# Direct head transposes, mask columns on VectorE and a reordered hand-over between two batches in a fused attention and snake-MLP kernel

## The chip, the cores and the metric

The kernel runs on one core of a Trainium2 chip. A core has a matrix engine (TensorE, PE in the profile, with its weight loads shown as PEld), VectorE (DVE), ScalarE (ACT), GpSimd (POOL) and SyncE (SP), each with an instruction queue of its own, and 16 DMA engines for transfers. The metric is the device time of one execution in microseconds. Before the change its median is 237.07 us over 8 runs (236.63 to 237.79).

## The reference

Four batches, 8 heads, 768 positions, head size 64. Each position attends to 8 memory keys of its batch and head and to a window around its own chunk of 32 positions; the result of all heads goes through a two-layer MLP with a snake activation.

```python
for c in range(nc):                       # chunks of 32
    l_start = max(0, c_start - 16); r_end = min(S, c_end + 8)
    k_full = np.concatenate([mem_k, k[:, :, l_start:r_end]], axis=2)
    v_full = np.concatenate([mem_v, v[:, :, l_start:r_end]], axis=2)
    scores = scale * np.matmul(q_c, k_full.transpose(0, 1, 3, 2))
    a = softmax(scores)
    out[:, :, c_start:c_end] = np.matmul(a, v_full)
x = out.transpose(0, 2, 1, 3).reshape(B * S, H * D)
h = x @ w_in                              # 512 -> 2048
s = np.sin(alpha * h)
g = h + s * s / (alpha + 1e-09)
return (g @ w_out).astype(np.float32)     # 2048 -> 512
```

## The kernel before

The work goes batch by batch, and the order of every engine's queue is the order of the program (L80 sets a manual schedule). Four kinds of work occur.

**Head (L173 to L438).** While the first loads arrive, `spin` (L167) runs matmuls on zeros. POOL issues the loads of k and q of batch 0 pair of heads by pair (`load_qk_pair`, L100; eight issues), builds the identity, builds the five mask columns `biasm` with a memset and eight affine selects (L189 to L199), and issues the 16 loads of v (`load_v`, L121). SP issues the loads of the memory keys and values and of alpha. For each pair of heads `pair_up` (L224) copies two heads side by side into `pr`; `t_k` and `t_q` (L239, L254) transpose six 128x128 blocks of it on PE and copy the result into `kTi` (DVE) and `qT` (ACT). Two zero matmuls follow each tile. ACT casts the memory values to bf16 (L418), and `put_memv` (L152) spreads them over `vw`. POOL then issues w_in in eight column blocks (L433), k and q of batch 1 (L435), w_out in four blocks of four ft (L436) and v of batch 1 in four loads (`load_v_all`).

**Attention (`burst`, L311).** Eight blocks of 96 queries. At step s, `qk_exp(s)` (L262) makes scores `sc` and three Exp on ACT with a mask column as bias; `pv(s - lag)` (L282) multiplies by v and the column of ones, and DVE makes the reciprocal and `x_blk`; `xt(s - lag - 1)` (L300) transposes `x_blk` and DVE copies it into `xT`. Batch 0 has lag 2 and one zero matmul per step. Later batches fill the gaps from a `Stream` (L20) of output matmuls of the batch before: at step s they take `shares[s]` of them, split in three places.

**First matmul stage (`l1`, L333).** For each of 16 column tiles ft of w_in: eight matmuls of `xT` (L341), Sin on ACT (L353; L350 in two halves), the square on the engine that a letter in the string at L466 names (A for ACT, D for DVE, P for POOL), and `gT` on DVE (L370, or L366 in halves). `finish` of one ft is called ahead of the matmuls of the next.

**Second matmul stage (`l2`, L376).** For each of six row tiles, 16 matmuls over ft (L398), a copy on DVE or ACT in turn (L405, L407) and a store. These are the units that the stream hands out. After batch 0's first stage come four such units (L481), and then the eight tiles of batch 1 transposed one by one with three units after each (`piece`, L482 to L484); `pair_to` (L454) makes their pair copies ahead, on DVE for even pieces of batch 1 and on POOL for odd ones.

PSUM holds three double banks (tag `big`: sc, ot, hT, tt_b) and two single banks (tag `sm`: z, xtp, o, hs, tt_a); a new tile waits for the last reader of the one whose place it takes. In batch 0 the transposed `x_blk` goes to a tile `xtp` of its own, in later batches into the place of `ot`.

Of the kernel before, what the change touches and what calls it, by code (L numbers as in the profile page):

```python
# [45 lines left out]
def kernel(  # L46
# [36 lines left out]
    ident = consts.tile([P, P], BF, name="ident")  # L83
    biasm = consts.tile([P, 5], F32, name="biasm")
    qT = consts.tile([P, HP, S], BF, name="qT")
    kTi = consts.tile([P, HP, KW], BF, name="kTi")
# [6 lines left out]
    memk_f = gp.tile([32, H, D], F32, name="memk_f", tag="gT")  # L93
    memv_f = gp.tile([P, B, H, D], F32, name="memv_f", tag="gT")
    w_in_sb = consts.tile([P, KT, d_ff], BF, name="w_in_sb")
# [89 lines left out]
    for b in range(B):  # L185
        nc.sync.dma_start(memk_f[NM * b:NM * b + NM], mem_k[b].rearrange("h n d -> n h d"))
    nc.sync.dma_start(memv_f[64:72].rearrange("n b h d -> n (b h) d"),
                      mem_v.rearrange("b h n d -> n (b h) d"))
    nc.gpsimd.memset(biasm[:], NEG)  # L189
    nc.gpsimd.memset(biasm[:, 0:1], 0.0)  # L190
    for c0, c1, thr, val in (
        (1, 2, 16, 0.0), (0, 2, 56, NEG), (0, 2, 64, 0.0), (0, 2, 72, NEG),
        (2, 4, 64, 0.0), (3, 4, 120, NEG), (4, 5, 32, 0.0), (4, 5, 96, NEG),
    ):
        nc.gpsimd.affine_select(
            out=biasm[:, c0:c1], in_=biasm[:, c0:c1],
            compare_op=ALU.is_gt, fill=val, base=thr,
            pattern=[[0, c1 - c0]], channel_multiplier=-1,
        )  # L199
    nc.scalar.copy(memk_bf[:], memk_f[:])  # L200
# [9 lines left out]

    def load_w_in(c):
        nc.gpsimd.dma_start(
            w_in_sb[:, :, 256 * c:256 * c + 256],
            moe_w_in[:, 256 * c:256 * c + 256].rearrange("(kt p) f -> p kt f", p=P),
        )

    def load_w_out(c):
        nc.gpsimd.dma_start(
            w_out_sb[:, 4 * c:4 * c + 4, :],
            moe_w_out[512 * c:512 * c + 512].rearrange("(ft p) o -> p ft o", p=P),  # L220
        )
# [16 lines left out]

    def t_k(kb, hp):  # L239
        t = t_tile()  # L240
        for r in range(6):
            nc.tensor.transpose(t[:, r, :], kb[:, r].rearrange("p e d -> p (e d)"), ident[:])  # L242
        nc.vector.tensor_copy(
            kTi[:, hp, 72:72 + 7 * 104].rearrange("p (s c) -> p s c", c=104)[:, :, 0:96]
            .rearrange("p s (a r) -> p s a r", r=6),
            t[:, :, 8:120].rearrange("p r (s a) -> p s a r", a=16),
        )
        for t0, c0 in ((0, 16), (120, 800)):
            nc.vector.tensor_copy(
                kTi[:, hp, c0:c0 + 48].rearrange("p (a r) -> p a r", r=6),  # L250
                t[:, :, t0:t0 + 8].rearrange("p r a -> p a r"),
            )

    def t_q(qb, hp):  # L254
        t = t_tile()
        for r in range(6):
            nc.tensor.transpose(t[:, r, :], qb[:, r].rearrange("p e d -> p (e d)"), ident[:])  # L257
        nc.scalar.copy(
            qT[:, hp, :].rearrange("p (a r) -> p a r", r=6), t[:].rearrange("p r a -> p a r")
        )  # L260

    def qk_exp(j):  # L262
        sc = big.tile([P, 2, 512], F32, name="sc", tag="big")
        for hp in range(HP):
            for e in range(2):
                nc.tensor.matmul(  # L266
                    sc[:, e, QW * hp:QW * hp + QW],
                    kTi[64 * e:64 * e + 64, hp, 104 * j:104 * j + P],
                    qT[64 * e:64 * e + 64, hp, QW * j:QW * j + QW],
                )  # L270
        pt = pts[state["n"] % NPT]
        state["n"] += 1
        for m in range(3):
            col = ((1 if j == 0 else 0), 4, (3 if j == NJ - 1 else 2))[m]
            nc.scalar.activation(  # L275
                pt[:, 0:H * QW].rearrange("p (g e c) -> p e g c", g=4, e=2)[:, :, :, 32 * m:32 * m + 32],
                sc[:, :, 0:4 * QW].rearrange("p g (e c) -> p g e c", e=4)[:, :, :, 32 * m:32 * m + 32],
                ACTF.Exp, bias=biasm[:, col:col + 1], scale=0.125,
            )
        return pt  # L280
# [19 lines left out]
    def xt(xT, j, x_blk, ot):  # L300
# [4 lines left out]
        for kt in range(KT):  # L305
            nc.tensor.transpose(  # L306
                xtp[:, kt, :], x_blk[:, 2 * kt:2 * kt + 2, :].rearrange("p e d -> p (e d)"), ident[0:QW, 0:QW]
            )
        nc.vector.tensor_copy(xT[:, :, QW * j:QW * j + QW], xtp)

    def burst(b, stream, shares, lag):  # L311

        xT = xp.tile([P, KT, S], BF, name="xT")
        ptl, xbl = {}, {}
        for s in range(NJ + lag + 1):
            n = shares[s] if s < len(shares) else 0
# [12 lines left out]
            stream.take((n + 2) // 3, True)  # L329
# [81 lines left out]

    first = [nc.vector.tensor_copy, nc.scalar.copy] * 2 + [nc.vector.tensor_copy] * 4
    prs = [pair_up(kq[n], 0, first[n]) for n in range(2)]
    for n in range(2 * HP):
        (t_k if n % 2 == 0 else t_q)(prs[n], n // 2)
        spin(2)
        if n == 3:
            nc.scalar.copy(memv_st[64:72], memv_f[64:72])  # L418
        if n == 1:
            mt = smp.tile([P, HP, 32], BF, name="mt", tag="sm")  # L420
            for hp in range(HP):
# [3 lines left out]
                    ident[0:32, 0:32])  # L425
        if n + 2 < 2 * HP:
            prs.append(pair_up(kq[n % 2], (n + 2) // 2, first[n + 2]))
        if n == 1:
# [13 lines left out]
    put_memk(1)  # L442
    put_memv(1)

    for i in range(B):
# [82 lines left out]
```

The softmax here doesn't subtract the row's maximum and nothing guards it: scores larger than these inputs give would overflow.

## Time and profile before

The profiled execution took 236.35 us; the span of its instructions is 234.6 us. The times by stage are in us from the start of the span.

| part | value |
|---|---|
| median of 8 runs | 237.07 us |
| profiled execution, its span | 236.35 us, 234.6 us |
| busy in the span: PE, DVE, ACT, POOL | 216.9, 160.8, 153.6, 73.0 us |
| first matmul (zeros), first Exp of batch 0 | 1.26, 16.73 |
| last xT copy of batch 0, ending | 28.93 |
| first gT copy chain of batch 0: first and last L370 of the stage | 32.12, ending 54.9 |
| first output matmul (L398) | 51.91 |
| first scores of batch 1, first Exp of batch 1 | 61.45, 63.02 |
| first L341 matmul of batch 1's first stage | 80.45 |

In the page's slices each digit is the busy share of one fortieth of the span, 5.9 us, in tenths. A row of the time line has start, duration, engine, line, operation, output and inputs, shapes and a count, and in brackets how long the engine was idle before it and what ended that. A busy PE is not a PE at its peak, since matmuls overlap in its pipeline; where the spacing of matmuls matters it is worked out from a group's duration.

### The profile page before, as it was taken

How to read it: one execution, taken by the hardware profiler on the slowest of the kernel's cores; microseconds unless marked ns; L12 is line 12 of the kernel's file. 1: busy time of each engine (PE TensorE's matmuls, PEld its weight loads, DVE VectorE, ACT ScalarE, POOL GpSimd, SP SyncE). 2: the span in 40 equal slices, each digit the busy share in tenths (PEclk: the TensorE clock that was granted, in tenths of full speed). 3: DMA queues.
4: the chain of work that ended last, by engine and by line, in shares of the span. 5: the costliest groups of instructions: out<-in, count | busy, mean ns of one | idle time of the engine just before them, and what ended most of it. 6: DMA issues, size and time to landing. Idle time of an engine off the chain costs nothing.

```text
span 234.6 us, 4467 instructions
## 1 busy us (share of the span) xinstructions
PE 216.9 (92%) x1759; PEld 122.2 (52%) x1785; DVE 160.8 (69%) x287; ACT 153.6 (65%) x237; POOL 73.0 (31%) x96
## 2 busy tenths in 40 slices
PE   7598799979989999998999999998999999899994
PEld 2255565545445566564455556564555555453453
DVE  3686969999338877988557598978566358775110
ACT  2589589984794397899664787779564676880000
POOL 7899965214822115139120115120000020010000
PEclk9999999999999999999999999999999999999999
DMA  6999999999999910019999101001111110101122
GB/s 79 159 135 83 153 188 204 208 205 152 142 221 153 158 45 3 0 46 137 178 142 121 48 0 45 3 3 42 48 45 48 46 45 3 45 0 45 61 75 89
DMA packets 53852, 21.11 MB, mean 90 GB/s; under 512 B 36296, under 2 KB 50888, under 8 KB 53832
## 3 DMA queue, kind: packets, MB, share of 16 engines
q0 software_dynamic: 47616, 14.40, 73.8%
q1 hardware_dynamic: 6216, 6.43, 9.3%
q8 instruction: 14, 0.23, 0.4%
q14 instruction: 6, 0.05, 0.1%
HBM read 28.91 MB, written 6.29 MB: 150 GB/s over the span
## 4 chain that ended last, share of the span: by engine, by line
PE 60%; DVE 14%; ACT 13%; issue 7%; DMA 3%; POOL 2%; POOLq 1%; DVEq 0%; ACTq 0%
PE o L398 29%; PE hT L341 19%; DVE gT L370 6%; ACT pt L275 4%; ACT u L353 4%; PE ot L288 3%; DVE s L362 3%; DMA q_bf<-in_q_dram 3%; PE sc L266 3%; ACT s L356 2%; PE ot L306 2%; DVE x_blk L293 2%; PE o L387 1%; PE tt_a L257 1%; PE tt_a L242 1%
## 5 line engine op out<-in xcount | busy, mean ns | idle before, releaser
L398 PE MATMUL o<-w_out_sb,gT 128*128 128x512 bf16 x343 | 93.1, 380 | 2.0 <-issue 0.5
L341 PE MATMUL hT<-xT,w_in_sb 128*128 128x384 bf16 x488 | 87.3, 326 | 3.9 <-DVE gT L370 3.6
L370 DVE SCALAR_TENSOR_TENSOR gT<-s,inv_alpha,hT 128x768 bf16<-128x768 f32 x61 | 60.8, 1013 | 21.4 <-ACT s L356 13.5
L353 ACT ACTIVATE u<-hT,alpha_sb 128x768 f32<-128x768 f32 x61 | 54.6, 897 | 25.7 <-PE hT L341 24.7
L341 PEld LDWEIGHTS <-w_in_sb 128*128 128x128 bf16 x512 | 49.3, 98 | 38.7 <-issue 4.8
L275 ACT ACTIVATE pt<-sc,biasm 128x256 bf16<-128x256 f32 x96 | 37.5, 492 | 12.5 <-PE sc L266 12.5
L398 PEld LDWEIGHTS <-gT 128*128 128x128 bf16 x368 | 31.9, 98 | 26.1 <-DVE gT L370 1.2
L358 POOL TENSOR_TENSOR s<-u 128x768 f32<-128x768 f32 x6 | 8.8, 1465 | 71.6 <-ACT u L353 61.3
L356 ACT ACTIVATE s<-u 128x768 f32<-128x768 f32 x34 | 28.7, 843 | 1.1
L362 DVE TENSOR_TENSOR s<-u 128x768 f32<-128x768 f32 x24 | 25.1, 1045 | 0.6 <-ACT u L353 0.5
L293 DVE TENSOR_TENSOR x_blk<-ot,rinv 96x512 bf16<-96x512 f32 x32 | 22.0, 686 | 1.1
L226 POOL COPY pr<-q_bf 128x768 bf16<-128x768 bf16 x12 | 10.1, 838 | 38.2 <-PE tt_a L242 22.8
L292 DVE RECIPROCAL rinv<-ot 96x8 f32<-96x8 f32 x32 | 6.4, 201 | 20.0 <-PE ot L288 19.6
L407 ACT COPY o_sb<-o 128x512 f32<-128x512 f32 x11 | 6.4, 585 | 20.0 <-PE o L398 20.0
L405 DVE COPY o_sb<-o 128x512 f32<-128x512 f32 x12 | 8.3, 688 | 15.4 <-PE o L398 15.1
L288 PEld LDWEIGHTS <-pt 128*128 128x128 bf16 x256 | 11.9, 98 | 7.2 <-issue 2.3
L171 PE MATMUL z<-zeros 128*128 128x512 bf16 x36 | 13.2, 451 | 1.5 <-DVE zeros L165 1.3
L288 PE MATMUL ot<-vw,pt 128*128 128x65 bf16 x256 | 13.0, 193 | 0.9 <-ACT pt L275 0.6
L266 PEld LDWEIGHTS <-kTi 64*128 64x128 bf16 x256 | 7.0, 94 | 13.0 <-issue 6.4
L266 PE MATMUL sc<-qT,kTi 64*128 64x96 bf16 x256 | 11.3, 205 | 1.9 <-ACT pt L275 1.2
L306 PEld LDWEIGHTS <-x_blk 96*128 96x128 bf16 x128 | 8.4, 97 | 6.6 <-DVE x_blk L293 1.6
L226 POOL COPY pr<-k_bf 128x768 bf16<-128x768 bf16 x8 | 6.6, 823 | 11.6 <-PE tt_a L257 5.8
(66 smaller groups left out, 180.9 us busy)
## 6 DMA issues: line engine op xcount, KB each, us to landing
out_dram<-o_sb SPq DMA_DIRECT2D x23, 256.0 KB, 2.6
k_bf<-in_k_dram POOLq DMA_DIRECT2D x3, 768.0 KB, 9.5
q_bf<-in_q_dram POOLq DMA_DIRECT2D x3, 768.0 KB, 13.3
vw<-in_v_dram POOLq DMA_DIRECT2D x6, 384.0 KB, 17.6
w_in_sb<-in_moe_w_in_dram POOLq DMA_DIRECT2D x8, 256.0 KB, 8.4
w_out_sb<-in_moe_w_out_dram POOLq DMA_DIRECT2D x4, 512.0 KB, 18.5
k_bf<-in_k_dram POOLq DMA_DIRECT2D x4, 192.0 KB, 5.9
q_bf<-in_q_dram POOLq DMA_DIRECT2D x4, 192.0 KB, 6.6
```

The costliest lines, as they stand in the source:

```text
L171: nc.tensor.matmul(z[:], zeros[:, 0:P], zeros[:])
L226: (eng or nc.gpsimd.tensor_copy)(pr[:].rearrange("p r e d -> p e r d"), src[:, 2 * hp:2 * hp + 2])
L266: nc.tensor.matmul(sc[:, e, QW * hp:QW * hp + QW], kTi[64 * e:64 * e + 64, hp, 104 * j:104 * j + P], qT[64 * e:64 * e + 64, hp, QW * j:QW ...
L275: nc.scalar.activation(pt[:, 0:H * QW].rearrange("p (g e c) -> p e g c", g=4, e=2)[:, :, :, 32 * m:32 * m + 32], sc[:, :, 0:4 * QW].rearra ...
L288: nc.tensor.matmul(otv[:, h // 4, h % 4, :], pt[:, QW * h:QW * h + P], vws[b % 2][:, h, j, 0:D + 1])
L293: nc.vector.tensor_tensor(out=x_blk[:].rearrange("p (g e) d -> p g e d", g=2), in0=otv[0:QW, :, :, 0:D], in1=rv.unsqueeze(3).to_broadcast( ...
L341: nc.tensor.matmul(hts[hf][:, 0:HALF], w_in_sb[:, kt, P * ft:P * ft + P], xT[:, kt, HALF * hf:HALF * hf + HALF], start=(kt == 0), stop=(kt ...
L353: nc.scalar.activation(u[:], hT[:, :, 0:HALF], ACTF.Sin, scale=alpha_sb[:, ft:ft + 1])
L356: nc.scalar.activation(s2[:], u[:], ACTF.Square)
L362: nc.vector.tensor_tensor(out=s2[:], in0=u[:], in1=u[:], op=ALU.mult)
L370: nc.vector.scalar_tensor_tensor(out=gv, in0=s2[:], scalar=inv_alpha[:, ft:ft + 1], in1=hT[:, :, 0:HALF], op0=ALU.mult, op1=ALU.add)
L398: nc.tensor.matmul(o[:], gT[:, ft, P * s:P * s + P], w_out_sb[:, ft, :], start=(ft == 0), stop=(ft == FT - 1),)
```

## The change

Everything lies in the head, in batch 0, and in the hand-over to batch 1.

- Head: the transposes read the loaded k and q directly, two of 64 columns (one per head, into the upper and lower half of the PSUM tile) in place of one of 128. The pair copies of batch 0 are gone.
- The memory values are loaded by POOL straight into `memv_st` in bf16; SP's load and ACT's cast are gone.
- The mask columns are made on DVE: sums over stretches of identity columns, three additions, one scale. Columns 2 and 3 change places.
- w_in comes in five loads in place of eight, w_out in two in place of four.
- Batch 0's attention: transposes one step later, two zero matmuls at steps 0 to 2 and 8 to 11, and the xT copies of blocks 4, 5 and 6 on ACT.
- First stage of batch 0: two squares fewer on ACT, two on POOL; the first pair copies of batch 1 move (two at ft 13, both on POOL).
- `put_memv(1)` moves behind the transposes of batch 1.
- The shares of output matmuls in batch 1's attention: 5, 5, 5, 4, 4, 4, 4, 4, 3, 3, 3, 3 in place of 3, 3, 3, 4, 4, 4, 4, 4, 4, 4, 5, 5.

```diff
-    nc.sync.dma_start(memv_f[64:72].rearrange("n b h d -> n (b h) d"),
-                      mem_v.rearrange("b h n d -> n (b h) d"))
-    nc.gpsimd.memset(biasm[:], NEG)
-    nc.gpsimd.memset(biasm[:, 0:1], 0.0)
-    for c0, c1, thr, val in (
...
+    nc.gpsimd.dma_start(memv_st[64:72].rearrange("n b h d -> n (b h) d"),
+                        mem_v.rearrange("b h n d -> n (b h) d"))
+    for c, (a, e) in enumerate(((0, 16), (16, 56), (64, 120), (120, P), (32, 96), (64, 72))):
+        nc.vector.tensor_reduce(
+            out=rows[:, c:c + 1], in_=ident[:, a:e], axis=mybir.AxisListType.X, op=ALU.add)
+    nc.vector.tensor_add(rows[:, 1:2], rows[:, 1:2], rows[:, 5:6])
+    nc.vector.tensor_add(rows[:, 0:1], rows[:, 0:1], rows[:, 1:2])
+    nc.vector.tensor_add(rows[:, 3:4], rows[:, 2:3], rows[:, 3:4])
+    nc.vector.tensor_scalar(
+        out=biasm[:], in0=rows[:, 0:5], scalar1=1.0, scalar2=-NEG, op0=ALU.subtract, op1=ALU.mult)
...
-            w_out_sb[:, 4 * c:4 * c + 4, :],
-            moe_w_out[512 * c:512 * c + 512].rearrange("(ft p) o -> p ft o", p=P),
+            w_out_sb[:, 8 * c:8 * c + 8, :],
+            moe_w_out[1024 * c:1024 * c + 1024].rearrange("(ft p) o -> p ft o", p=P),
...
+    def turn(src, hp):
+
         t = t_tile()
         for r in range(6):
-            nc.tensor.transpose(t[:, r, :], kb[:, r].rearrange("p e d -> p (e d)"), ident[:])
+            if src.shape[1] == 6:
+                nc.tensor.transpose(t[:, r, :], src[:, r].rearrange("p e d -> p (e d)"), ident[:])
+            else:
+                for e in range(2):
+                    nc.tensor.transpose(t[64 * e:64 * e + 64, r, :], src[:, 2 * hp + e, r, :], ident[:])
+        return t
...
-        nc.vector.tensor_copy(xT[:, :, QW * j:QW * j + QW], xtp)
+        (nc.scalar.copy if ot is None and j in (4, 5, 6) else nc.vector.tensor_copy)(
+            xT[:, :, QW * j:QW * j + QW], xtp)
...
-        for s in range(NJ + lag + 1):
+        back = lag + (2 if b == 0 else 1)
+        for s in range(NJ + back):
...
-                spin(1)
+                spin(1 if 3 <= s < NJ else 2)
...
-            if 0 <= s - lag - 1 < NJ:
-                xt(xT, s - lag - 1, *xbl.pop(s - lag - 1))
+            if 0 <= s - back < NJ:
+                xt(xT, s - back, *xbl.pop(s - back))
...
-    first = [nc.vector.tensor_copy, nc.scalar.copy] * 2 + [nc.vector.tensor_copy] * 4
-    prs = [pair_up(kq[n], 0, first[n]) for n in range(2)]
     for n in range(2 * HP):
-        (t_k if n % 2 == 0 else t_q)(prs[n], n // 2)
+        (t_k if n % 2 == 0 else t_q)(kq[n % 2], n // 2)
         spin(2)
-        if n == 3:
-            nc.scalar.copy(memv_st[64:72], memv_f[64:72])
...
-    for c in range(8):
-        load_w_in(c)
+    for c0, c1 in ((0, 256), (256, 512), (512, 1024), (1024, 1536), (1536, 2048)):
+        load_w_in(c0, c1)
     kq_next = load_qk(1)
-    for c in range(4):
+    for c in range(2):
         load_w_out(c)
     load_v_all(1)
...
-    put_memv(1)
...
-                pieces.append(pair_up(*srcs[len(pieces)], nc.vector.tensor_copy if i == 0 and len(pieces) % 2 == 0 else None))
+                pieces.append(pair_up(*srcs[len(pieces)], nc.vector.tensor_copy if i == 0 and len(pieces) in (2, 4, 6) else None))
...
-            sq = ("ADADADAAADADADAA" if i == 0 else "ADAAPDADADAPADAD")[ft]
+            sq = ("ADADADADPDPAADAA" if i == 0 else "ADAAPDADADAPADAD")[ft]
...
-            if i == 0 and ft == 14:
-                pair_to(3)
+            if i == 0 and ft == 13:
+                pair_to(2)
...
+                put_memv(1)
...
-                xT = burst(i + 1, stream, (3, 3, 3, 4, 4, 4, 4, 4, 4, 4, 5, 5), 3)
+                xT = burst(i + 1, stream, (5, 5, 5, 4, 4, 4, 4, 4, 3, 3, 3, 3), 3)
```

More of the change, by code (lines that the diff above doesn't have):

```diff
@@ L84 @@
     biasm = consts.tile([P, 5], F32, name="biasm")
+    rows = consts.tile([P, 6], F32, name="rows")
     qT = consts.tile([P, HP, S], BF, name="qT")
@@ L93 @@
     memk_f = gp.tile([32, H, D], F32, name="memk_f", tag="gT")
-    memv_f = gp.tile([P, B, H, D], F32, name="memv_f", tag="gT")
     w_in_sb = consts.tile([P, KT, d_ff], BF, name="w_in_sb")
@@ L186 @@
         nc.sync.dma_start(memk_f[NM * b:NM * b + NM], mem_k[b].rearrange("h n d -> n h d"))
-    nc.sync.dma_start(memv_f[64:72].rearrange("n b h d -> n (b h) d"),
-                      mem_v.rearrange("b h n d -> n (b h) d"))
-    nc.gpsimd.memset(biasm[:], NEG)
-    nc.gpsimd.memset(biasm[:, 0:1], 0.0)
-    for c0, c1, thr, val in (
[L192 to L199, printed above, removed]
+    nc.gpsimd.dma_start(memv_st[64:72].rearrange("n b h d -> n (b h) d"),
[8 more added lines that the diff above has]
+        out=biasm[:], in0=rows[:, 0:5], scalar1=1.0, scalar2=-NEG, op0=ALU.subtract, op1=ALU.mult)
     nc.scalar.copy(memk_bf[:], memk_f[:])
@@ L209, with load_w_in @@
         nc.vector.memset(pt[:, H * QW:H * QW + 32], 0.0)
-    def load_w_in(c):
+    def load_w_in(c0, c1):
         nc.gpsimd.dma_start(
-            w_in_sb[:, :, 256 * c:256 * c + 256],
-            moe_w_in[:, 256 * c:256 * c + 256].rearrange("(kt p) f -> p kt f", p=P),
+            w_in_sb[:, :, c0:c1],
+            moe_w_in[:, c0:c1].rearrange("(kt p) f -> p kt f", p=P),
         )
@@ L237, in t_tile, with t_k @@
         return big.tile([P, 6, P], BF, name="tt_b", tag="big")
-    def t_k(kb, hp):
+    def turn(src, hp):
         t = t_tile()
         for r in range(6):
-            nc.tensor.transpose(t[:, r, :], kb[:, r].rearrange("p e d -> p (e d)"), ident[:])
+            if src.shape[1] == 6:
[4 more added lines that the diff above has]
+        return t
+    def t_k(kb, hp):
+        t = turn(kb, hp)
         nc.vector.tensor_copy(
@@ L254, in t_q @@
     def t_q(qb, hp):
-        t = t_tile()
-        for r in range(6):
-            nc.tensor.transpose(t[:, r, :], qb[:, r].rearrange("p e d -> p (e d)"), ident[:])
+        t = turn(qb, hp)
         nc.scalar.copy(
@@ L273, in qk_exp @@
         for m in range(3):
-            col = ((1 if j == 0 else 0), 4, (3 if j == NJ - 1 else 2))[m]
+            col = ((1 if j == 0 else 0), 4, (2 if j == NJ - 1 else 3))[m]
             nc.scalar.activation(
@@ L425 @@
                     ident[0:32, 0:32])
-        if n + 2 < 2 * HP:
-            prs.append(pair_up(kq[n % 2], (n + 2) // 2, first[n + 2]))
-        if n == 1:
             nc.vector.tensor_copy(memkT[:], mt[:])
```

## The prediction

> **What bounds the kernel now.** I read the page's slices first, then busy time by stage, then the time lines of the three places where the stages hand over. All times are from the start of the 234.6 us span.
>
> ```profile
> PE   7598799979989999998999999998999999899994
> DVE  3686969999338877988557598978566358775110
> PEclk9999999999999999999999999999999999999999
> DMA  6999999999999910019999101001111110101122
> ```
>
> From slice 14 (82 us) on PE is nearly full and the transfers are rare. Before that PE has holes, and the transfer engines are full from 6 to 82 us. The clock is never below full, so extra zero matmuls have no clock to win here. The change touches only the first 80 us; later work just moves with them.
>
> ```profile
> 17.00:29.00 12.00, 9.79 (x164) 6.36 (x162) 9.49 (x27) 9.93 (x25) 12.00 (x17) 1.00 1.28 114
> 32.00:43.00 11.00, 10.69 (x66) 6.25 (x64) 10.61 (x13) 10.78 (x16) 6.03 (x7) 1.00 1.36 202
> 43.00:55.00 12.00, 10.31 (x67) 5.93 (x66) 11.36 (x15) 10.00 (x14) 2.49 (x3) 1.00 1.36 201
> 55.00:61.50 6.50, 6.31 (x57) 3.73 (x57) 5.80 (x15) 2.63 (x4) 3.82 (x5) 1.00 4.18 123
> 61.50:69.20 7.70, 6.58 (x79) 3.03 (x79) 1.58 (x4) 7.55 (x18) 4.05 (x5) 1.00 1.47 193
> 69.20:80.40 11.20, 10.91 (x137) 6.59 (x140) 9.04 (x24) 5.47 (x11) 2.22 (x3) 1.00 2.62 174
> ```
>
> Columns: stretch, length, then busy us of PE, PE loads, DVE, ACT, POOL. Batch 0's attention is split between ACT (its 24 Exps stand without a gap from 16.73 to 25.64) and DVE. Its first matmul stage (32 to 55) is bound by DVE (10.61 of 11, 11.36 of 12) with ACT close behind. The transposes for batch 1 (55 to 61.5) are PE's. Batch 1's attention begins as ACT's (7.55 of 7.70, PE has room) and turns into PE's at 69.2.
>
> The handover that decides this forecast is that into the first output matmuls:
>
> ```profile
> L218 POOL DMA_DIRECT2D w_out_sb<-in_moe_w_out_dram x4: 740/741/752, 31.6 to 35.6; - x4
> DMA to landing us min/median/max: 16.6/18.5/20.3
> ...
> 54.45 0.81 PE L398 MATMUL o<-w_out_sb,gT 128*128 128x512 bf16 x3
> 55.09 0.50 PE L242 MATMUL tt_a<-ident,pr 128*128 128x128 bf16 x6
> 55.43 0.87 PE L398 MATMUL o<-w_out_sb,gT 128*128 128x512 bf16 x3
> ```
>
> Four w_out loads of four ft each: the first lands at 31.6 + 16.6 = 48.2, the last at 35.6 + 20.3 = 55.9, so they land 2.57 us apart. The output matmuls go 4, 3, 3, 3: ft 12 is the third of the group at 55.43, that is 55.86 (216 ns each). The last load lands just then. Weights and PE arrive together.
>
> **Head: transposes straight from the loads.** The pair copies go (0.36 us on DVE, 0.83 on ACT), and ACT's 1.89 us cast of memv. In their place stand 12 transposes of 64 columns for 6 of 128.
>
> ```profile
> 14.57 0.36 DVE L226 COPY pr<-q_bf 128x768 bf16<-128x768 bf16 x1 [0.37 <-DMA q_bf<-in_q_dram]
> 14.99 0.37 PEld L257 LDWEIGHTS <-pr 128*128 128x128 bf16 x6 [0.28 <-DVE pr L226]
> 15.03 0.50 PE L257 MATMUL tt_b<-ident,pr 128*128 128x128 bf16 x6
> 15.57 0.80 ACT L258 COPY qT<-tt_b 128x768 bf16<-128x768 bf16 x1
> ```
>
> Six in 0.50 us, the last one 0.22 long: 58 ns apart. No row has a 64-column transpose. Lower end: the 64-row sc matmuls, 8 in 0.34 us with 0.205 for one, 19 ns apart. Upper end: a load (98 ns) and a stream (58) one after the other, 156. I take 58, the nearest row: 12 x 58 = 0.70 us, with two zero matmuls (0.43) 1.13 us a tile. The last loads arrive about 1.0 us apart, so PE falls slightly behind: from q of pair 1 (10.6; I take 10.3, since memv's 64 KB no longer run among these 192 KB loads, 64/192 of 1.0 us) four tiles give 14.8, and the last transpose ends at 14.8 + 0.70 + 0.16 = 15.66 instead of 15.53. **Head: +0.1**, from -0.8 (19 to 29 ns, bound by the load) to +8.5 (156 ns: 5.9 + 7 x 2.3 + 2.0 = 24.0).
>
> [...]
>
> The mask columns leave POOL (0.16 + 0.10 + 1.94 us) and become 10 small DVE instructions. Nearest rows: a small memset 0.07, the 128x16 reciprocal 0.255; 0.7 to 2.6 us. DVE is idle 2.83 us before its first copy at 5.92, and its first work afterwards is a kTi copy after 6.6. Nothing, at both ends; without that cover at most 2.6.
>
> memv is now a ninth POOL load (0.7 us of issue) before the 16 v loads. The waits view shows a POOL issue held until the transfer eight places before it has landed (w_out after w_in, vw after k_bf and q_bf). So v loads 2 to 6 wait for q and k to land, until about 14.8, and of the 2.2 - 0.7 = 1.5 us only some 0.35 reaches the first w_in issue (22.26). put_memv(0) runs at 15.96 on DVE; memv lands behind the last q (14.5) and ahead of that.
>
> **Attention of batch 0.** Three of eight xT copies (0.34 us, 0.26 in a row) go to ACT, after its last Exp; nearest ACT rows 0.37 (256 elements) and 0.59 (512), so 1.1 to 1.8 us and then the table load of 1.28, against 3.37 us of ACT idle before the first Sin: hidden. DVE loses 0.78. But steps 3 to 5 are paced by ACT (each pv waits for an Exp), the zero matmuls double at the end (0.22 each), and each takes the PSUM slot of an xT copy two steps back, behind which pv or the next transpose queues. Step by step I get the last xT within 0.1 of where it was relative to the first Exp. **0**, from -0.8 (all of DVE's) to +0.9 (four doubled matmuls exposed).
>
> **First matmul stage.** Two squares leave ACT (2 x 0.84) for POOL (1.47 each), whose issues now end near 39 because its last two vw loads wait for w_in rather than k and q (42.06 and 45.97 before). DVE keeps six squares and all 16 gT; it loses its one wait on ACT (0.42) and one or two copies (0.54 together, of which 0.3 returns after the stage). A DVE square beside a POOL copy takes 1.22 instead of 0.95. **-0.5**, from -1.0 to +0.5 (both POOL squares late by 0.5).
>
> [...]
>
> **The wait that the change adds.** w_out comes in two loads of eight ft. So ft 8, at 54.45 + 0.22 = 54.67 before, now needs what came with the last load. Sum for that landing: 55.9 - 0.35 (earlier start) - 0.25 (w_in in 512-column blocks: 256 KB take 1.33 us by the POOL waits, w_out's 512 KB 2.57, 3% of 8 us) - 0.2 (three issues fewer beside the transfers; no row prices it, bounds 0 and 0.5) = 55.1. PE arrives at 54.67 + 0.1 - 0.5 = 54.3, waits 0.8, and behind it in PE's order queue six transposes and the groups between them, for which ACT, DVE and all of batch 1's attention wait. So head and first stage are worth nothing: this point is 55.1 - 54.67 = +0.4, and as DVE meanwhile catches up, PE's wait of 0.31 at 57.74 on DVE's kTi goes. **Start of batch 1's attention: +0.1**, from -0.8 (no wait) to +0.7 (landing unchanged).
>
> put_memv(1) (1.22 on DVE) moves behind the transposes, where DVE is idle 4.79 before 65.80: nothing; uncovered 1.22. The 512-column block of w_in that ft 4 waits for holds the two blocks that landed by 31.60 and 32.86, and ft 4 starts near 34: nothing.
>
> **Batch 1's attention.** Shares 5,5,5,4... for 3,3,3,4..., 47 both: six matmuls (6 x 0.216 = 1.3 us) move forward into steps 0 to 2. There ACT rules until 69.2 and PE waits:
>
> ```profile
> 66.94 0.35 PE L266 MATMUL sc<-qT,kTi 64*128 64x96 bf16 x8 [0.53 <-ACT pt L275]
> 67.22 0.39 PE L398 MATMUL o<-w_out_sb,gT 128*128 128x512 bf16 x1
> 68.04 0.40 PE L288 MATMUL ot<-vw,pt 128*128 128x65 bf16 x8 [0.43 <-ACT pt L275]
> ```
>
> sc(3) moves from 64.72 to 66.0, still ahead of the Exp before it (ends 66.9). The last four steps, bound by PE, lose those six. With three each they come near DVE's 1.10 per step, and between the last pv and its transpose only four are left (1.05 with a transpose, against 1.4 for pv, reciprocal, x_blk), so 0.3 comes back. **-1.0**, from -0.2 to -1.3.
>
> **Sum.** 0.1 - 1.0 = -0.9: from the profiled 236.35 (span 234.6) to 235.45; from the median of 237.07, to which runs compare and which lies 0.7 above that execution, to 236.2. A measurement tells about 0.2% (0.5 us) from no change.
>
> **Forecast and rivals.** (1) As above, chance 0.50, 235.7 to 236.7. (2) w_out does not bind: it lands by 54.2, and head, stage and attention keep another 0.9: 235.3 (234.7 to 235.6). For it: smaller issue count, longer packets; against: full transfer engines. 0.20. (3) The early matmuls do not do what they are for, because sc(1) to sc(3) come late for ACT, or w_out lands unchanged (+0.7): 237.0 (236.6 to 237.6), 0.17. (4) Slower: 64-column transposes keep to the load's 98 ns row. A tile takes 1.61 us, eight from 5.9 end at 5.9 + 7 x 1.61 + 1.18 + 0.16 = 18.5, 3.0 late; PE reaches ft 8 at 54.3 + 2.9 = 57.2, past the w_out wait. That is +2.5 there, less the 0.31, less 1.0: 238.3, from 237.6 to 243.8 at 156 ns. It turns slower from 87 ns, where the last transpose ends at 17.4. 0.13.
>
> Faster: 0.47 + 0.20 + 0.03 = 0.70; same: 0.03 + 0.11 + 0.03 = 0.17; slower: 0.03 + 0.10 = 0.13. The range 234.9 to 237.7 leaves out the ends of (2) and most of (4), under 2 in 10.
>
> **What would show it.** First Exp near 16.7 to 16.9 (under 16.3: halves run side by side; over 18: rival 4). A wait of L398 in the second group after the stage, ending on a w_out transfer, near 55. sc of batch 1 near 61.5, and its first L341 near 79.6 instead of 80.4. If the POOL squares begin after 46 the queue was not freed and the stage is longer.

## The result and the profile after

After: median 236.09 us (24 runs, 235.57 to 239.52); before: 236.99 (64 runs). Ratio 0.9953, interval 0.9938 to 0.9969: faster by 0.9 us, and 236.2 was forecast. The profiled execution after took 236.38 us with a span of 234.4. The page's slices after:

```profile
PE   7898999888999999998999999998999999899994
DVE  5467669998747987988557698977566358775110
...
PEclk9999999999999999999999999999999999999999
DMA  6999999999999910019998101001111110101112
```

PE is fuller than before in the first three slices (7, 8, 9 for 7, 5, 9) and there is nothing new after slice 14. The same stages as in the table of before, from the answer on stretches (stretch, length, busy us of PE, PE loads, DVE, ACT, POOL, clock):

```profile
16.00:28.30 12.30, 10.92 (x170) 6.66 (x170) 8.44 (x23) 10.73 (x28) 12.30 (x18) 1.00 1.22 101
28.30:51.80 23.50, 21.36 (x127) 12.41 (x128) 19.75 (x24) 19.36 (x26) 10.99 (x9) 1.00 1.26 205
51.80:62.00 10.20, 8.92 (x76) 5.32 (x76) 9.04 (x20) 5.00 (x7) 4.60 (x6) 1.00 3.20 144
62.00:69.70 7.70, 7.54 (x83) 3.58 (x83) 2.61 (x6) 7.62 (x18) 5.50 (x5) 1.00 1.26 202
69.70:80.20 10.50, 9.84 (x131) 6.03 (x134) 8.53 (x23) 5.48 (x11) 1.60 (x2) 1.00 2.65 160
```

In batch 1's attention (62.00 on) PE is now busy 7.54 of 7.70 us where it was 6.58: the early matmuls fill its room beside ACT. The marks between the stages, each the start of a first instruction, say where time went:

| mark (us) | before | after | stage's length, before and after |
|---|---|---|---|
| first Exp | 16.73 | 15.72 | head: -1.0 |
| first matmul of batch 0's first stage that waits for the last xT | 28.98 | 28.34 | attention: 12.25, 12.62 |
| first output matmul | 51.91 | 51.85 | first stage: 22.93, 23.51 |
| first scores of batch 1 | 61.45 | 62.00 | batch 1's transposes: 9.54, 10.15 |
| first hT of batch 1 | 80.45 | 80.24 | batch 1's attention: 19.00, 18.24 |
| end of the span | 234.6 | 234.4 | the rest: 154.14, 154.20 |

The head gains 1.0, the next three stages give back 1.6, batch 1's attention gains 0.8. The rest takes 154.13 to 154.20 in every kernel of this study, so each difference arises before batch 1's first stage.

**How the clock comes in.** The spans of these two profiles differ by 0.2 us (their times by nothing), the medians by 0.9. Each execution has its span and mean granted clock on record. Of 93 executions of before beside and among the experiments, in three jobs, 42 have a mean clock of 0.984 to 0.993, and 51 are at 0.998 or more; these full-clock ones have a median time of 236.89 us and a median span of 234.8 (234.1 to 236.8). After shows 0.993 in 3 of 36; the other 33 have 236.07 us and a span of 234.1 (233.5 to 234.9). Pooled like this, the change is worth 0.8 us at full clock (0.7 in the span). But before's full-clock median is not the same in the three jobs (236.41, 236.82 and 237.04 us), and only one of these ran both kernels. There the eleven full-clock executions of each have 236.41 and 235.96 us, with spans of 234.2 and 234.0: 0.45 in the time and 0.2 in the span, as in the profiled pair. All executions of that job differ by 1.0, so more than half of the gain there is that after is rarely slowed. The share of the clock in the 0.9 lies between these two readings and is not known closer. What a reduced clock is shows the profile of one kernel below (e5), in two stretches:

```profile
9.20:12.60 3.40, 3.40 (x24) 1.98 (x22) 2.19 (x8) 1.63 (x2) 2.97 (x7) 0.50 1.30 199
29.60:33.00 3.40, 3.35 (x11) 1.57 (x11) 1.70 (x2) 0.90 (x1) 2.69 (x3) 0.51 1.38 180
```

The seventh figure of a row is the granted clock: half, for 3.4 us at a time. One such stretch makes a mean of 0.993 (1.7 of 235), two make 0.986. Before's executions with 0.990 to 0.993 have a median of 237.31 us (25 of them), those with 0.984 to 0.986 of 238.58 (17).

### The profile page after: what moved, and what is told of

Same layout as the page of the kernel before. It is cut to its first block, busy times and chain, and to the rows that moved or that the text cites. A ratio compares the mean times of both kernels' runs of the same rounds, so it can differ in the third digit from the quotient of the medians.

```text
span 234.4 us, 4551 instructions
## 1 busy us (share of the span) xinstructions
PE 219.0 (93%) x1812; PEld 122.6 (52%) x1841; DVE 159.3 (68%) x287; ACT 150.4 (64%) x235; POOL 74.1 (32%) x85
## 4 chain that ended last, share of the span: by engine, by line
PE 59%; DMA 15%; POOL 8%; DVE 7%; issue 6%; ACT 3%; POOLq 1%; DVEq 0%; ACTq 0%
PE o L404 30%; PE hT L347 18%; DMA w_out_sb<-in_moe_w_out_dram 12%; DVE gT L376 3%; PE sc L270 3%; DMA k_bf<-in_k_dram 3%; PE ot L292 2%; PE tt_a L241 2%; POOL vw L129 2%; ACT u L359 2%; PE ot L310 2%; DVE s L368 2%; PE o L393 1%; POOL vw L125 1%; DVE x_blk L297 1%
## 5 line engine op out<-in xcount | busy, mean ns | idle before, releaser
L364 POOL TENSOR_TENSOR s<-u 128x768 f32<-128x768 f32 x8 | 12.5, 1568 | 75.5 <-ACT u L359 65.1
L362 ACT ACTIVATE s<-u 128x768 f32<-128x768 f32 x32 | 27.0, 844 | 1.3 <-DVE gT L376 0.3
L368 DVE TENSOR_TENSOR s<-u 128x768 f32<-128x768 f32 x24 | 25.9, 1078 | 0.7 <-ACT u L359 0.5
L171 PE MATMUL z<-zeros 128*128 128x512 bf16 x41 | 14.5, 446 | 1.3 <-DVE zeros L165 1.2
L270 PEld LDWEIGHTS <-kTi 64*128 64x128 bf16 x256 | 6.8, 94 | 12.4 <-issue 5.9
L241 PEld LDWEIGHTS <-pr 128*128 128x128 bf16 x144 | 10.1, 98 | 5.2
```

Source lines behind the costliest of these rows:

```text
L171: nc.tensor.matmul(z[:], zeros[:, 0:P], zeros[:])
L241: nc.tensor.transpose(t[:, r, :], src[:, r].rearrange("p e d -> p (e d)"), ident[:])
L270: nc.tensor.matmul(sc[:, e, QW * hp:QW * hp + QW], kTi[64 * e:64 * e + 64, hp, 104 * j:104 * j + P], qT[64 * e:64 * e + 64, hp, QW * j:QW ...
L362: nc.scalar.activation(s2[:], u[:], ACTF.Square)
L368: nc.vector.tensor_tensor(out=s2[:], in0=u[:], in1=u[:], op=ALU.mult)
```

## The experiments

The theory after the result: the head is 1.0 us quicker because half-width transposes cost no more than full ones (twelve take 0.53 us, six full ones 0.50); the squares on POOL, the w_out wait and the doubled zero matmuls each give some of it back; the early shares bring 0.8. The rivals: the zero matmuls hold the clock up, and that is the gain; or w_out's landing rules alone, so that nothing ahead of it counts.

**Both kernels again** (e0 is after, e4 is before, unchanged).

> The changed kernel once more, as the measure for the three beside it: 0.995 of the kernel before (236.0 to 236.4 us). Both theories expect PE to wait about 1.2 us at ft 8 of the first output matmuls for the second half of w_out, and that half to land near 55.5 us; if the wait is a matter of one execution it will be under 0.5 here.

> The kernel before, once more, for a second profile of it: 1.000 within 0.3%. The profiled executions of before and after differ by nothing (236.35 and 236.38) while their medians differ by 1.1 us; if the profile of before on record was a fast one, this one's span is 234.6 to 236, and the stretch in which it is longer says what varies between executions.

Measured: after 236.02 against 237.03, ratio 0.9952 (0.9919 to 0.9985); before 237.88 against 237.26, 0.9991 (0.9957 to 1.0025). The marks of their profiles lie within 0.25 us of the first ones, and the wait for w_out is 1.17 us again. The differences by stage repeat.

**e1: w_out in four loads again.**

```diff
-            w_out_sb[:, 8 * c:8 * c + 8, :],
+            w_out_sb[:, 4 * c:4 * c + 4, :],
...
-    for c in range(2):
+    for c in range(4):
         load_w_out(c)
```

> The changed kernel with w_out in four loads of four ft again. Theory W (the merged load holds PE, and behind it the transposes of batch 1): the wait of 1.2 us at ft 8 goes or shrinks to 0.2 at ft 12; VectorE is next late (its kTi copies start at 55.1 whatever PE does), so 0.5 of the 1.2 is won in the start of batch 1's attention: 235.4 to 235.7, that is 0.5 below the changed kernel. Rival D (VectorE is the bound there anyway): the wait goes and the scores of batch 1 still start at 61.9 to 62.0; no change against the changed kernel, within 0.2.

Measured: 240.05 us, ratio 1.0103 (1.0062 to 1.0144): 4 us slower than after, which no theory had. POOL's time line in e1 (start, us, engine, line, operation; in brackets the wait before it):

```profile
40.29 0.78 POOL L145 DMA_DIRECT2D vw<-in_v_dram  x1 [2.50 <-DMA k_bf<-in_k_dram]
44.16 0.84 POOL L148 DMA_DIRECT2D vw<-in_v_dram  x1 [3.09 <-DMA q_bf<-in_q_dram]
45.02 2.90 POOL L364 TENSOR_TENSOR s<-u 128x768 f32<-128x768 f32 x2
```

With two loads more, eight issues before the last two vw loads stand batch 1's k and q again, whose landing holds POOL until 44.16. The two squares queue behind, from 45.02 instead of 41.20. DVE's gT waits for them, and PE for DVE; e1's PE time line and clock slices:

```profile
47.60 7.98 PE L347 MATMUL hT<-xT,w_in_sb 128*128 128x384 bf16 x32 [3.54 <-DVE gT L376]
```

```profile
PEclk9999999859999999999999999999999999999999
```

PE idles 3.54 us, from 44.06 to 47.60, and within this gap the clock falls to half, from 46.1 to 53.0: 32 matmuls take 7.98 us. All six executions have 0.984 to 0.993. So fewer w_out loads are what lets the squares go to POOL. The two edits belong together, and the price of the one can't be had by undoing it alone.

**e2: no squares on POOL. e7: that, and w_out in four loads.**

```diff
-            sq = ("ADADADADPDPAADAA" if i == 0 else "ADAAPDADADAPADAD")[ft]
+            sq = ("ADADADAAADADADAA" if i == 0 else "ADAAPDADADAPADAD")[ft]
```

> The changed kernel with the squares of batch 0 on ACT and DVE as before (no square on POOL in that stage). Theory P (a POOL square and a DVE square exclude each other): the POOL square of 2.29 us and the DVE square of 2.03 us are gone, DVE squares take 0.95 to 1.22, the stage from first hT to first output matmul takes 22.9 in place of 23.5 us and PE gets to ft 8 at 53.7 instead of 54.3; but it then waits 1.8 us for w_out, so the time is that of the changed kernel within 0.3. Rival (the POOL squares relieve ACT and are worth it): the stage gets longer, 24 us or more, and the time rises by 0.5.

> The changed kernel with w_out in four loads and the old squares. Theories W and P together: the stage is 0.6 shorter and VectorE's copies of batch 1 start that much earlier, and only ft 12 waits for w_out (landing 55.5 against 54.9): 235.0 to 235.4, about 0.9 below the changed kernel. If W holds and P does not: as with four loads alone. If neither: as the changed kernel.

Measured: e2 235.35, 0.9914 (0.9876 to 0.9951); e7 235.09, 0.989 (0.9853 to 0.9927). Without the squares on POOL the time is 0.7 us lower, more than expected; w_out in four loads brings another 0.3, by medians of two jobs. In e2 the stage takes 22.68 us instead of 23.51, and PE comes to ft 8 at 53.15 instead of 54.41 and waits longer. PE's time line of e2:

```profile
52.77 0.38 PE L404 MATMUL o<-w_out_sb,gT 128*128 128x512 bf16 x1
54.74 0.59 PE L404 MATMUL o<-w_out_sb,gT 128*128 128x512 bf16 x2 [1.59 <-DMA w_out_sb<-in_moe_w_out_dram]
```

The load is there at 54.7, against 55.5 in after, and batch 1's scores start at 61.16 instead of 62.00: 0.84 earlier, as is the matmul behind the wait (54.74 for 55.58). So the shorter stage goes into the wait, and what reaches batch 1 in this profile is the earlier landing: here the rival holds that w_out's landing fixes the point. It isn't shown why the load lands earlier, nor by what path squares on POOL would hold it back; the first Exp, ahead of the edit, already stands at 15.29 for 15.72.

**e3: the old shares.**

```diff
-                xT = burst(i + 1, stream, (5, 5, 5, 4, 4, 4, 4, 4, 3, 3, 3, 3), 3)
+                xT = burst(i + 1, stream, (3, 3, 3, 4, 4, 4, 4, 4, 4, 4, 5, 5), 3)
```

> The changed kernel with the old shares of output matmuls in batch 1's attention (3,3,3,4,...,5,5). Theory S (the early matmuls fill holes that PE has while ACT rules): the stretch from the first scores of batch 1 to the first hT of its matmul stage is 19.0 in place of 18.2 us, the time 0.7 to 0.8 above the changed kernel (236.8). Rival (the gain came from elsewhere): within 0.2 of the changed kernel.

Measured: 236.72, 0.9978 (0.9952 to 1.0005), all twelve executions at full clock; after beside it 236.02. Batch 1's attention takes 19.02 us instead of 18.24. The shares are worth 0.7 to 0.8.

**e5: before, with w_out in two loads.**

```diff
-            w_out_sb[:, 4 * c:4 * c + 4, :],
+            w_out_sb[:, 8 * c:8 * c + 8, :],
...
-    for c in range(4):
+    for c in range(2):
         load_w_out(c)
```

> The kernel before with w_out in two loads of eight ft and nothing else. Theory W: PE waits at ft 8 (54.67) for a landing at 55.9, 1.2 us, and the transposes behind it come late; VectorE's copies, which were the next bound, absorb some: 0.6 to 1.2 us slower (237.6 to 238.2). Rival D: no change within 0.2.

Measured: 238.06, 1.0015 (0.9984 to 1.0046), not apart from before by itself. Its eleven full-clock executions have 237.93 (span 235.8) against before's 236.89 (234.8): +1.0. Its profile was the one slowed execution, so PE came late to ft 8 and shows no wait. That only 1 of 12 was slowed, with before's head, is not explained.

**e6: before, with the new head alone** (direct transposes, the six `rows` sums for the mask, memv on POOL's queue; squares, loads, attention and shares as before).

> The kernel before with the new head alone: direct transposes, mask columns on DVE, memory values loaded by POOL. Twelve 64-column transposes take 0.53 us as in the changed kernel, the first Exp comes at 15.7 in place of 16.7. Theory W: the attention's end is 1.0 earlier, the first matmul stage too, but w_out's last quarter still lands at 55.5, so ft 12 waits 0.6: 0.2 to 0.5 faster than before. Rival (head gain is kept): 0.9 to 1.0 faster.

Measured: 235.74, 0.9918 (0.9886 to 0.9951), eight of eight at full clock: the head alone brings 1.1 us against the full-clock executions of before in its job (236.82), more than the whole change at full clock (0.45 to 0.8). First Exp at 15.40, first output matmul at 50.88, batch 1's scores at 60.70 (61.45 before). Theory W's wait is there, 0.49 us for w_out at ft 12, but the gain is above its 0.2 to 0.5: of the 1.33 us by which the first Exp is earlier, 0.75 reach batch 1's scores. What PE does in its head, 5.7 to 9.1 and 9.2 to 12.6 us, in e6:

```profile
5.70:9.10 3.40, 2.81 (x34) 1.11 (x32) 2.13 (x6) 0.80 (x1) 3.40 (x6) 1.00 1.34 184
9.20:12.60 3.40, 3.36 (x54) 1.73 (x54) 1.51 (x6) 1.53 (x2) 2.81 (x5) 1.00 1.32 187
```

In before PE is busy 1.65 and 2.31 us of these two.

**f1: after with one zero matmul per step. f2: before with two of them past the last block.**

```diff
-                spin(1 if 3 <= s < NJ else 2)
+                spin(1)
```

```diff
-                spin(1)
+                spin(1 if s < NJ else 2)
```

> The changed kernel with one zero matmul at every step of batch 0's attention, as before the change. Theory C (the doubled zero matmuls at the attention's end keep the granted clock up there): at full clock it is within 0.2 of the changed kernel or 0.1 faster, but in a good part of the executions, a third or more, the granted clock falls under 0.995 and the time goes to 237.5 and above. Rival H (the denser head keeps the clock, not the zero matmuls): no more than 1 execution in 10 falls under 0.995, the median is that of the changed kernel, 236.0, within 0.2.

> The kernel before with two zero matmuls in place of one at the last steps of batch 0's attention only. Theory C: executions at two windows of half clock (0.986, 14 of 64) vanish, at most one window is left (the one in the head), the median falls by 0.3 to 0.6 to 236.6 to 236.9. Rival H: half of the executions still fall under 0.9965, 0.986 among them, no change.

Measured: f1 235.8, 0.9928 (0.9897 to 0.9959), 11 of 12 at full clock; f2 237.55, 0.9997 (0.9962 to 1.0032), 5 of 12. The doubled zero matmuls don't hold the clock: fewer of them leave it up, more don't mend before. The theory of the clock by these zero matmuls falls. In f1 the attention of batch 0 takes 12.02 us (end of the last xT copy from the first Exp), 12.56 in after: the doubled ones cost 0.5 there. The time is not apart from after's (235.8 for 236.02 in another job). In f1's profile batch 1's scores start 0.48 earlier than in after, which is how much earlier w_out lands (PE goes on at 55.10 for 55.58).

**f4: the POOL squares two tiles apart** (they stay at ft 8 and 10, with ACT instead of DVE at 7 and 9, and DVE instead of ACT at 11).

```diff
-            sq = ("ADADADADPDPAADAA" if i == 0 else "ADAAPDADADAPADAD")[ft]
+            sq = ("ADADADAAPAPDADAA" if i == 0 else "ADAAPDADADAPADAD")[ft]
```

> The changed kernel with the squares of ft 7 and 9 on ACT, so that no DVE square stands beside the two POOL squares. If a DVE instruction with two SBUF inputs and a POOL instruction shut each other out, both POOL squares now take 1.47 us (2.29 and 1.47 before) and the 2.03 us DVE square is gone; the stage from first hT to first output matmul takes 22.6 in place of 23.5 us. The time is then that without POOL squares or 0.2 better (235.1 to 235.4). If POOL squares are slow for a reason of their own, one of them stays above 2 us and the time stays at 236.0.

Measured: 236.11, 0.9943 (0.9914 to 0.9972), as after. POOL's time line, then DVE's, in f4:

```profile
43.76 1.46 POOL L364 TENSOR_TENSOR s<-u 128x768 f32<-128x768 f32 x1 [5.95 <-ACT u L359]
46.37 1.47 POOL L364 TENSOR_TENSOR s<-u 128x768 f32<-128x768 f32 x1 [1.15 <-ACT u L359]
```

```profile
45.25 1.94 DVE L376 SCALAR_TENSOR_TENSOR gT<-s,inv_alpha,hT 128x768 bf16<-128x768 f32 x2 [1.10 <-POOL s L364]
47.87 1.01 DVE L376 SCALAR_TENSOR_TENSOR gT<-s,inv_alpha,hT 128x768 bf16<-128x768 f32 x1 [0.67 <-POOL s L364]
```

With no DVE square beside them the POOL squares take 1.46 and 1.47, and the DVE square of 2.03 is gone (longest 1.37). But DVE now waits 1.10 and 0.67 us for POOL, and the stage is 23.48 as in after, not the 22.6 expected; the half clock that this profile has, from 9.0 to 12.4, lies ahead of it. POOL's 1.47 us in the chain is late by itself where ACT's 0.84 was not.

**f3: head, w_in blocks and shares, without the rest** (e7, and batch 0's attention as before).

```diff
-        (nc.scalar.copy if ot is None and j in (4, 5, 6) else nc.vector.tensor_copy)(
-            xT[:, :, QW * j:QW * j + QW], xtp)
+        nc.vector.tensor_copy(xT[:, :, QW * j:QW * j + QW], xtp)
...
-        back = lag + (2 if b == 0 else 1)
+        back = lag + 1
...
-                spin(1 if 3 <= s < NJ else 2)
+                spin(1)
```

> The changed kernel without its three costs: w_out in four loads, squares on ACT and DVE, batch 0's attention as before (one zero matmul a step, transposes one step behind pv, all xT copies on DVE). Theory: the last xT stands 12.2 us after the first Exp in place of 12.56, the wait for w_out at ft 12 grows to some 1 us, since the landing (55 us) now holds the output matmuls; 234.6 to 235.1, no more than 0.4 below the run with four loads and old squares (235.1). Rival (the attention's changes are worth something): 235.4 or more.

Measured: 234.97, 0.9891 (0.9843 to 0.994), the lowest median here and below both kernels; e7, in another job, lies 0.1 above. First output matmul 50.90, scores of batch 1 60.78, its first stage 79.03 (80.24 in after). PE's time line of f3:

```profile
54.59 0.59 PE L403 MATMUL o<-w_out_sb,gT 128*128 128x512 bf16 x2
55.56 0.38 PE L403 MATMUL o<-w_out_sb,gT 128*128 128x512 bf16 x1 [0.37 <-DMA w_out_sb<-in_moe_w_out_dram]
```

The wait on w_out is 0.37 us, at ft 12, not the 1 us expected.

**The landing of w_out and the start of batch 1, over all profiles.** Seven profiles have a wait of PE for w_out. In them batch 1's first scores stand at a fixed distance behind the first matmul after the wait:

| profile | loads of w_out | wait (us) | matmul after it | scores of batch 1 | between |
|---|---|---|---|---|---|
| after | 2 | 1.17 | 55.58 | 62.00 | 6.42 |
| e0 | 2 | 1.17 | 55.42 | 61.84 | 6.42 |
| e2 | 2 | 1.59 | 54.74 | 61.16 | 6.42 |
| e3 | 2 | 1.55 | 55.42 | 61.84 | 6.42 |
| f1 | 2 | 0.91 | 55.10 | 61.52 | 6.42 |
| e6 | 4 | 0.49 | 55.48 | 60.70 | 5.22 |
| f3 | 4 | 0.37 | 55.56 | 60.78 | 5.22 |

PE came there as early as 53.15 (e2) and as late as 54.41 (after), and it made no difference: while PE waits, the landing alone sets the start, and a quicker head, attention or stage only lengthens the wait. With two loads the start is 1.20 us further behind the landing than with four. The other profiles have no such wait: PE came no earlier than the load. In them the scores follow the first output matmul: by 9.54 us in before, e4, e5 and f2, by 9.72 in e7 and f4, by 10.08 in e1. In after it is 10.15. So of the 1.17 us that PE waits in after, the start of batch 1 loses about 0.43, an estimate from f4, which differs from after in squares alone.

## Why the prediction was right, point by point

The number was right, and so was the mechanism that it rests on: the wait for w_out, and not the work ahead of it, sets the start of batch 1's attention, and the early shares shorten that attention. That the number is so close is luck in part. Summed over the two profiles the change is worth 0.2 us, not 0.9: batch 1's attention starts at +0.55 instead of +0.1, and is 0.76 shorter instead of 1.0. The medians show 0.9 because before runs at a reduced clock more often, which the prediction had not reckoned with, and because executions at full clock spread, which stays open. Three terms ahead of the wait were off as well, in both directions, and nearly cancel.

**Head, +0.1 forecast, -1.0 measured.** The mis-sized term is the 58 ns per transpose of 64 columns. The time line after (start, us, ..., in brackets the wait):

```profile
14.04 0.53 PE L244 MATMUL tt_b<-ident,q_bf 128*64 128x128 bf16 x12
...
14.61 0.80 ACT L262 COPY qT<-tt_b 128x768 bf16<-128x768 bf16 x1 [1.19 <-PE tt_b L244]
...
15.72 0.47 ACT L279 ACTIVATE pt<-sc,biasm 128x256 bf16<-128x256 f32 x1 [0.31 <-PE sc L270]
```

Twelve take 0.53 us, where six of 128 columns took 0.50: 12 x 58 would be 0.70. With the last one's 0.22 taken off, that is (0.53 - 0.22) / 11 = 28 ns for each. In the trace the two halves of a pair start 3 to 4 ns apart and most pairs 56 ns apart, which is the spacing of the full transposes in before: the halves run side by side. That is near the lower end that the prediction had kept (19 to 29 ns). With 28 ns PE doesn't fall behind the loads. The last tile starts as its load lands, at 14.04, where in before that load was there at 14.57 and the transposes began at 15.03, after the pair copy: half of the gain is the copy, half the earlier landing, of which the prediction had 0.3 and then lost it to PE. The gain lies beyond its lower end of -0.8, and why the load lands 0.53 earlier has no run of its own. The weight loads cost nothing extra either: the twelve together take 0.36 us, the six before took 0.37. A single load is no shorter for half the columns (106 to 110 ns for 64, 95 to 99 for 128), but the loads of the two halves overlap: the first two, of 106 ns each, start 3 ns apart.

**Attention of batch 0, 0 forecast, +0.36 measured.** The estimate took "the last xT within 0.1 of where it was". The end of it after, on ACT:

```profile
25.18 0.48 ACT L313 COPY xT<-xtp 128x384 bf16<-128x384 bf16 x1 [0.59 <-PE xtp L310]
26.28 0.48 ACT L313 COPY xT<-xtp 128x384 bf16<-128x384 bf16 x1 [0.62 <-PE xtp L310]
27.10 0.48 ACT L313 COPY xT<-xtp 128x384 bf16<-128x384 bf16 x1 [0.34 <-PE xtp L310]
```

Each copy waits for PE, where two zero matmuls (0.60 us) stand in every step: PE paces the end, not ACT. f1 takes one away and the stage has 12.02; behind the wait for w_out neither shows. Forecast's upper end, four doubled matmuls exposed (0.9), holds this.

**First stage, -0.5 forecast, +0.6 measured.** The failed step is "a DVE square beside a POOL copy takes 1.22 instead of 0.95". The row that it went by, and the copy beside it, in before:

```profile
46.80 0.83 POOL L226 COPY pr<-q_bf 128x768 bf16<-128x768 bf16 x1
47.24 1.22 DVE L362 TENSOR_TENSOR s<-u 128x768 f32<-128x768 f32 x1
```

After, on POOL, on DVE, and on PE:

```profile
41.20 2.29 POOL L364 TENSOR_TENSOR s<-u 128x768 f32<-128x768 f32 x1 [3.12 <-ACT u L359]
44.20 1.47 POOL L364 TENSOR_TENSOR s<-u 128x768 f32<-128x768 f32 x1 [0.71 <-ACT u L359]
```

```profile
41.22 0.95 DVE L368 TENSOR_TENSOR s<-u 128x768 f32<-128x768 f32 x1
...
44.46 2.03 DVE L368 TENSOR_TENSOR s<-u 128x768 f32<-128x768 f32 x1
```

```profile
47.66 4.36 PE L347 MATMUL hT<-xT,w_in_sb 128*128 128x384 bf16 x24 [1.60 <-DVE gT L376]
```

The two squares that began together, at 41.20 and 41.22, took 2.29 and 0.95: POOL's 1.47 and the whole of DVE's on top, less 0.13. At 44.46 DVE was the one that waited (2.03): its 0.95 and the 1.21 us that POOL's square, ending at 45.67, still had to run, again less 0.13. PE stood still for 1.60 us afterwards. So in both pairs the two squares took nearly the sum of their times, as if one ran after the other. The row with 1.22 could not price that: when its square began, at 47.24, the copy had only 0.39 us left (it ends at 47.63). f4 shows that this is not all of it: with the squares parted DVE waits 1.10 and 0.67 us for POOL instead, and the stage is no shorter. e2, without squares on POOL, has the stage 0.8 shorter and the time 0.7 lower, in its profile by the earlier landing.

**The w_out wait, 0.8 forecast, 1.17 measured.** The loads' issue and landing, and PE there:

```profile
L215 POOL DMA_DIRECT2D w_out_sb<-in_moe_w_out_dram x2: 958/958/959, 27.1 to 28.0; - x2
...
DMA to landing us min/median/max: 22.7/25.1/27.5
```

```profile
54.03 0.38 PE L404 MATMUL o<-w_out_sb,gT 128*128 128x512 bf16 x1
55.58 0.59 PE L404 MATMUL o<-w_out_sb,gT 128*128 128x512 bf16 x2 [1.17 <-DMA w_out_sb<-in_moe_w_out_dram]
56.01 0.50 PE L241 MATMUL tt_a<-ident,pr 128*128 128x128 bf16 x6
```

Second load: 28.0 + 27.5 = 55.5 (55.1 forecast); PE is at ft 8 at 54.4 (54.3 forecast), and the six transposes queue behind. The mechanism and its place stand. The term that is off is the landing, 0.4 late: the first w_in issue came 0.54 earlier than before (21.72), more than the 0.35 forecast, but the landing only 0.34, so that nothing is seen of the other two terms, 0.25 for larger w_in blocks and 0.2 for fewer issues, which no run here shows. Batch 1's attention starts +0.55 instead of +0.1. The landings of the same two loads spread as much between profiles (54.7 in e2), unexplained, so that a difference of 0.4 can't be put down to one cause. That PE was in time is luck: a head 1.1 better than forecast paid for a stage 1.1 and an attention 0.4 worse. With the forecast's +0.1 for the head PE would have come to ft 8 at about 55.5, just as the load lands (an estimate, 54.4 + 1.1). The page's chain of waits shows the load too:

```profile
PE o L404 30%; PE hT L347 18%; DMA w_out_sb<-in_moe_w_out_dram 12%; DVE gT L376 3%; PE sc L270 3%; DMA k_bf<-in_k_dram 3%; PE ot L292 2%; PE tt_a L241 2%; POOL vw L129 2%; ACT u L359 2%; PE ot L310 2%; DVE s L368 2%; PE o L393 1%; POOL vw L125 1%; DVE x_blk L297 1%
```

Its 12% are the transfer's whole 27.5 us, since the chain runs back along it; what a quicker landing could win is less than the wait of 1.17, by the estimate above 0.43.

**Batch 1's attention, -1.0 forecast, -0.76 measured** (e3: 0.7 to 0.8). Right, somewhat large.

**"No clock to win here"** was right for zero matmuls (f1, f2) and wrong of the clock: one profile at 1.00 doesn't say that all executions are. Nor is the start at full speed: after's zero matmuls up to 5.0 us lie 0.43 apart (0.23 later on) and its first twelve transposes, at 5.57, take 0.85 us, as at half clock in f4. The page shows 1.00 there only because the record of the clock begins at 6.58. PE then waits 0.84 us for q, so it costs after nothing. "The transfers are rare" from slice 14 on is misread for slices 18 to 21, which are full (9); nothing here rests on it.

Of the rivals, (2) falls for the changed kernel, where w_out binds; times like its 235.3 come with the squares on DVE and ACT (e2, 235.35) and with w_out in four loads as well (e7 and f3, 235.0 to 235.1), and in e2 and f3 w_out still binds. (3) falls: the early matmuls work (e3), and w_out landed between the 55.1 of the forecast and before's 55.9. (4) falls with the 0.53 us of a tile.

**Open:** the profiles add up to -0.2, the full-clock medians to -0.8 over all jobs and to -0.45 in the one job that has the clocks of both kernels; the profiled before lies 0.2 under its full-clock median span and the profiled after 0.3 over its own, and where in the stages that spread arises is not shown. What spreads before's full-clock spans over 2.7 us (after's over 1.4) is open, and so is why e5 was slowed so rarely. The new head goes with the steadier clock: leaving out e1, kernels with it were below 0.997 in 8 of 102 executions, those with the old head in 50 of 117. That the density of its PE work is the reason is argued, not tested by itself, and e5, with the old head and 1 of 12, speaks against it.

The clock records of the traces bear on it. The stretches at half clock are 3.4 us long (e5, f4), and 6.9 in e1, twice that; the one at full clock in before and in after is 228.69 us long, as long as 67 of 3.413 each. The point they are counted from differs between executions: the record begins, at full clock, at 5.74 us in before and 6.58 in after, at 4.23 in e2 and 9.87 in e4. Cut into such stretches of 3.413 us from there, the stretch ahead of each fall to half clock has little work on PE: 0.94 us of 3.41 in f2, 1.27 and 2.23 in e5, 1.30 in e1, 1.61 in e7, 1.74 in f4. But others as sparse were followed by full clock (1.68 in before, 1.73 in f1, 1.48 later on in f4), so there is no sharp bound by these figures. That the stretches lie differently each time fits that a sparse head is hit in some executions only.

## What to carry to other kernels

At a hand-over between stages, find the arrival that ends the wait before pricing the work ahead of it: while PE waited for w_out, the next stage began 6.42 us behind the load, whether PE had been there 0.9 or 1.6 us before. Price an instruction on a second engine by its duration there in the chain that waits for it, and by what the two engines do to each other, before counting what it frees on the first: with two squares moved to an idle POOL the stage became 0.8 us longer. Where edits share a queue, take them back together: w_out in four loads is 0.3 us better without the POOL squares (medians of two jobs) and 4 us worse with them. Read the clock over many executions before saying that there is none to win.

## What the runs showed of the hardware

- Transposes of 64 columns into the upper and the lower half of a PSUM tile, in turn, ran in pairs: the two of a pair start 3 to 4 ns apart, most pairs 56 ns apart like full transposes (after), 12 in 0.53 us. At half clock (the head of f4's profile) 12 take 0.85.
- The clock fell to half for 3.4 us at a time: in the head (e5 9.2 to 12.6, f4 9.0 to 12.4, both at 0.50) in some executions of a kernel, in e5 once more from 29.6 to 33.0 (0.51), and in e1 for 6.9 us, 46.1 to 53.0 (0.50 and 0.51), from within a gap of PE of 3.54 us. No long gap of PE stood ahead of the two in e5: at most 1.25 and 0.47 us. Where the record begins differs between executions (5.74 us in before, 6.58 in after, 4.23 in e2, 9.87 in e4).
- A square of 128x768 f32 took 1.46 to 1.47 us on POOL with none on DVE beside it (f4), 2.29 when one of DVE began 0.02 us after it (after); DVE's took 0.95, and 2.03 when it began 0.26 us after one of POOL (after).
- The last two vw issues on POOL's queue were held until the transfer eight issues earlier had landed, and POOL's own work behind them too. In before, k of batch 1 lands at 41.8 (28.2 + 13.6) and q at 45.7 (29.5 + 16.2), and the vw issues eight behind them start at 42.06 and 45.97, after waits of 2.50 and 3.12 us. In e1 they stand eight behind k and q as well and wait 2.50 and 3.09 us for them; in after, with two w_out loads fewer, they stand eight behind w_in loads and wait 1.23 and 1.83 us for those.
